# Four weight halves converted beside the attention and kept in memory, an integer mantissa, and a third bank for the first layer

## The chip, the core and the metric

The kernel runs on one core of one Trainium2 chip. Its engines work side by side, each on its own instructions in a fixed order: PE (TensorE) multiplies, PEld loads its weights, DVE (VectorE), ACT (ScalarE) and POOL (GpSimd) do element work, SP (SyncE) starts transfers. PE writes into eight PSUM banks of 128x512 floats, which DVE and ACT read and POOL does not use here. The metric is device time in microseconds; lower is better.

## The reference, cut to what matters

```python
B, H, S, D = 8, 8, 576, 64             # q, k, v; block-causal mask, blocks of 64
scores = q @ k.T / sqrt(D);  attn = softmax(mask(scores));  x = attn @ v
x = x.transpose(0, 2, 1, 3).reshape(4608, 512)
h = x @ w_in                            # w_in 512 x 2048
g = max(h, 0) + alpha * min(h, 0)       # alpha: one number for each of 2048 units
out = g @ w_out                         # w_out 2048 x 512
```

w_in and w_out come to the kernel as doubles. It has to make floats of them itself, with integer operations on the two 32-bit words of each double.

## The kernel before

**Stages.** The 32 pairs of heads (four to a batch of 576 tokens) run one after the other; the scores, softmax, transposes and values of each are `query_tile` and `values`. The 2048 hidden units are 16 blocks of 128, numbered f. For f = 0 to 5 both layers run in chunks of 256 tokens (`chunk_a`: `ffn1` at L518 for the first layer, `ffn2` at L555 for the second) beside the attention, and three of these chunks are left when it ends, near 598 us. Here they are called A chunks. Blocks 6 to 15 follow in nine chunks of 512 tokens (C chunks), two blocks at a time: `pair1` makes seven products of 128x256 (L596) and joins them on DVE (L605, L609); `activate` applies alpha (ACT L529, DVE L531, ACT L535, POOL L538); `ffn2` multiplies by w_out.

**Conversion.** `to_f32` turns one half (w_in or w_out of one f, 128x512) into floats. SP loads the doubles into `raw` (L414). DVE masks the exponent (L416), ACT scales it into a bank (L419), DVE adds the sign (L421) and masks the mantissa into a second bank (L425), ACT makes a float of that (L428), DVE adds the low word (L430) and multiplies by the exponent (L433) into `m`. So a half costs five DVE and two ACT instructions. Then `split` makes a high part on ACT (L438) and a low part on POOL (L439). There are two `raw` tiles, and two `m` tiles until the attention is over, then four.

**When.** The 12 halves of f = 0 to 5 are converted in the first 100 us (`first_weights`). Of the 20 later halves, w_in of f = 6 and 7 are converted early too (priority `SOON`, in the trace from 105.65 us on) and stay in the two `m` tiles. The other 18 are converted from 605 us to 707 us, beside the last three A chunks and the first C chunk (`later_weights`), together with w_in's sums on POOL (L455).

**Order.** All instructions are recorded with engine, cost and priority (`Plan.op`), and `Plan.schedule` lists them by a model of the costs: on each engine the ready instruction of lowest priority number goes first. The chip then runs each engine's list as it stands. Tiles and banks are claimed in this plan. Banks have quotas: 6 for attention (`att`), 1 for hidden values (`hp`), 1 for sums (`acc`) during the attention; after it `hp` is HT, `acc` is AM, and the conversions get WB = 4 (`words`).

```python
BANKS, HB, AB, HT, AM, AT, WB = 6, 1, 1, 2, 2, 4, 4
plan.quota["hp"] += HT - HB
```

Of the kernel before, what the change touches and what calls it, by code (L numbers as in the profile page):

```python
# [9 lines left out]
F32 = mybir.dt.float32  # L10
F32R = mybir.dt.float32r
BF16 = mybir.dt.bfloat16
I32 = mybir.dt.int32
U32 = mybir.dt.uint32
AF = mybir.ActivationFunctionType
ALU = mybir.AluOpType
# [4 lines left out]
NP = H // 2  # L21
NPAIR = B * NP
DM, DF, DO = H * D, 2048, 512
P = 128
NCC = DM // P
NF = DF // P
TOK = B * S
FA = 6
# [6 lines left out]
RING = 2 * S  # L35

HALVES = (((4, 3, 2), (2 * P, S, 1)), ((1, 0), (0, 2 * P, 0)))
BANKS, HB, AB, HT, AM, AT, WB = 6, 1, 1, 2, 2, 4, 4
C0, C1 = 3.0, 4.0
WARM, WARM_END = 10, 3400  # L40
TICK, FULL_COLUMNS, SP0 = 3413.33, 3060, 700
# [3 lines left out]
E0, E1 = -4.0, 1.0  # L45
FP = -1
XP = 2.0
SOON, XB = 150, 1006.7
FEW = 12
BEGIN = {"SP": SP0, "ACTQ": SP0, "POOLQ": SP0, "PE": WARM_END, "ACT": 2000, "DVE": 1500, "POOL": 1700}  # L50
# [177 lines left out]
def c_dve(n):  # L228
    return 65 + n / 0.96


def c_dve2(n):
    return 150 + n / 1.92


def c_act(n, sbuf=False):
    return (93 if sbuf else 51) + n / 1.2
# [35 lines left out]
def attn_ffn(ctx, tc, qT, kT, vT, w_in, w_out, alpha, out):  # L273
    nc = tc.nc

    const = ctx.enter_context(tc.tile_pool(name="const", bufs=1))
    dram = ctx.enter_context(tc.tile_pool(name="dram", bufs=1, space=bass.MemoryType.DRAM))
# [20 lines left out]

    xd = dram.tile([P, NCC, TOK], F32, name="xd")
    part = dram.tile([TOK, DO], F32, name="part")  # L300

    wraw = ctx.enter_context(tc.tile_pool(name="wraw", bufs=1))

# [8 lines left out]
    att = ExitStack()  # L312
# [36 lines left out]
    op = plan.op  # L349
# [52 lines left out]
    def to_f32(src, prio, after=(), use="att", early=None):  # L402

        raw, eb, fb, mb = Buf("raw"), Buf("bank", use), Buf("bank", use), Buf("m")

        def low():
            return raw().rearrange("p (n t) -> p n t", t=2)[:, :, 0].bitcast(U32)

        def high():
            return raw().rearrange("p (n t) -> p n t", t=2)[:, :, 1]  # L410

        def e():
            return eb().bitcast(I32)
        op("SP", 512, lambda: nc.sync.dma_start(out=raw(), in_=src), r=after, w=[raw], prio=prio if early is None else early)  # L414

        op("DVE", c_dve2(512), lambda: nc.vector.tensor_scalar(  # L416
            out=mb().bitcast(I32), in0=high(), scalar1=0x7FF00000, scalar2=None, op0=ALU.bitwise_and),
            r=[raw], w=[mb], claim=[fb, eb], prio=prio)
        op("ACT", c_act(512, True), lambda: nc.scalar.activation(  # L419
            out=e(), in_=mb().bitcast(I32), func=AF.Relu, bias=ebias, scale=8.0), r=[mb], w=[eb], prio=prio)  # L420
        op("DVE", c_dve(512), lambda: nc.vector.scalar_tensor_tensor(  # L421
            out=e(), in0=high(), scalar=-2 ** 31, in1=e(), op0=ALU.bitwise_and, op1=ALU.bitwise_or),
            r=[raw], w=[eb], prio=prio)

        op("DVE", c_dve(512), lambda: nc.vector.tensor_scalar(  # L425
            out=fb().bitcast(I32), in0=high(), scalar1=0xFFFFF, scalar2=0x100000, op0=ALU.bitwise_and, op1=ALU.bitwise_or),
            r=[raw], w=[fb], prio=prio)
        op("ACT", c_act(512), lambda: nc.scalar.activation(out=fb(), in_=fb().bitcast(I32), func=AF.Copy, scale=2.0 ** -20),  # L428
           w=[fb], prio=prio)
        op("DVE", c_dve(512), lambda: nc.vector.scalar_tensor_tensor(  # L430
            out=mb(), in0=low(), scalar=2.0 ** -52, in1=fb(), op0=ALU.mult, op1=ALU.add),
            r=[raw, fb], w=[mb], prio=prio)
        op("DVE", c_dve(512), lambda: nc.vector.tensor_tensor(out=mb(), in0=mb(), in1=eb(), op=ALU.mult), r=[eb], w=[mb], prio=prio)  # L433
        return mb, mb

    def split(src, hi, lo, n, r, hk, lk, claim, on, prio):
# [20 lines left out]

    w1s, w2s = {}, {}

    def later_weights(prio):  # L460


        for f in range(FA, NF, 2):
            W = w1s[f] = Buf("w1")

            ms = [to_f32(w_in[f + i].bitcast(I32), *((prio(f), ["att"], "words") if f > FA else (SOON, [], "att"))) for i in range(2)]
            (m0, w0), (m1, w1) = ms
            sb = Buf("ws")
            q11, q12 = ((m0, lambda j=j, w0=w0: w0()[:, 256 * j:256 * j + 256]) for j in range(2))
            q21, q22 = (((m1, j), lambda j=j, w1=w1: w1()[:, 256 * j:256 * j + 256]) for j in range(2))  # L470
            s1, s2 = (((sb, j), lambda j=j, sb=sb: sb()[:, 256 * j:256 * j + 256]) for j in range(2))
            pr = prio(f)
            add("POOL", 256, s1, q21, q22, ALU.add, pr, [m1, "att"])
            add("POOL", 256, s2, s1, q11, ALU.subtract, pr)
            add("POOL", 256, q21, q11, q21, ALU.subtract, pr)
            for src, r, at, n, on in ((w0, [m0, "att"], 0, 512, "POOL"), (w1, [m1, q21[0]], 2, 512, "POOL"),
                                      (lambda sb=sb: sb(), [s1[0], s2[0]], 4, 512, "POOL")):
                hi, lo = ((lambda x=x, at=at, n=n, W=W: W()[:, x, 256 * at:256 * at + n]) for x in range(2))
                split(src, hi, lo, n, r, (("w1", f, at), "h"), (("w1", f, at), "l"), [W], on, pr)
            add("POOL", 256, s2, q12, s2, ALU.subtract, pr)  # L480
            hi, lo = ((lambda x=x, W=W: W()[:, x, 6 * 256:]) for x in range(2))
            split(s2[1], hi, lo, 256, [s2[0]], (("w1", f, 6), "h"), (("w1", f, 6), "l"), [W], "POOL", pr)
            for i in range(2):
                W = w2s[f + i] = Buf("w2")
                mb, w = to_f32(w_out[f + i].bitcast(I32), prio(f) + .5, ["att"], "words")
                hi, lo = ((lambda x=x, W=W: W()[:, x, :]) for x in range(2))
                split(w, hi, lo, 512, [mb], (("w", f + i, 1), "h"), (("w", f + i, 1), "l"), [W], "POOL", prio(f) + .5)

# [496 lines left out]
    for p in range(NP):  # L985
        pr = E1 * (p - NP) + E0
# [6 lines left out]
    for p in range(NPAIR):  # L993
        if p == NV:
            op("NONE", 0, end_plain, ends=("vraw0",), prio=-100, then=lambda: rooms("pt", ("V", 1, [5, 4, D], F32R)),
               w=[("PT", i, h, j, x) for i in range(3) for h in range(2) for j in range(6) for x in range(2)])
        pr = p * 5
        qk_parts, v_parts = prep(p, pr - 4.5) if p else rest(pr - 4.5)
        k = 0
        for js, span in HALVES[:1] if p < NP else HALVES:  # L1000
            for j in js:
                query_tile(p, qk_parts, j, pr + k)
                k += 1
            values(p, v_parts, [span], pr + k + .5)
        if p % NP == NP - 1:
            b = p // NP
            spill(b, p * 5 + 20)
            if p == NPAIR - 1:
                break
            while done + CHA <= (b + 1) * S:  # L1010
                chunk_a(done)
                done += CHA
# [92 lines left out]
```

## Time and profile before

| | |
|---|---|
| median of 3 runs | 1147.3 us (1147.26 to 1149.0) |
| the profiled execution | 1147.15 us, of which its span is 1145.4 us |
| PE, PEld busy | 1119.7 us (98%), 999.0 us (87%) |
| DVE, ACT, POOL busy | 844.1 us (74%), 730.1 us (64%), 612.1 us (53%) |
| transfers | 145.86 MB, nearly all from SP's queue |

Read it by stretches: the start to about 110 us, the attention to 598 us, a passage from there to about 690 us in which the later weights are converted, and the C chunks to the end. The span is what the profile covers; the profiled execution's own time is 1.75 us longer. Matmuls overlap, so that a busy PE can be slower than PE at its best; the number of matmuls in a stretch tells more.

### The profile page before, as it was taken

To read this page: it belongs to the slowest core of one execution; us is meant where nothing else is said; L and a number is where in the kernel's file an instruction comes from. 1 tells how busy PE (TensorE), PEld (TensorE's weight loads), DVE (VectorE), ACT (ScalarE), POOL (GpSimd) and SP (SyncE) were. 2 spreads that over 40 slices of the span, in tenths; PEclk is the share of its full clock that TensorE was granted. 3 is DMA by queue.
4 is the path that set the end of the run, shared out by engine and by line. 5 is a ranking of instruction groups with operands and counts; after the bars stand their busy time and mean duration, and the time that the engine had idled before them with its cause. 6 is when DMAs were issued, how large, how long until landed. Compare 5 with 4: busy or idle time off the path is not lost. (4 is left out here: it accounts for less than half of the span.)

```text
span 1145.4 us, 22040 instructions
## 1 busy us (share of the span) xinstructions
PE 1119.7 (98%) x7288; PEld 999.0 (87%) x7288; DVE 844.1 (74%) x1968; ACT 730.1 (64%) x1950; POOL 612.1 (53%) x769
## 2 busy tenths in 40 slices
PE   7998999999999999999999989999999999999998
PEld 5666999999989999999998878988898889989887
DVE  8888899887887777778868999655657474656554
ACT  6887898987777887788865766443434343343432
POOL 5756556555565455556448987342425343342522
PEclk9999999999999999999999999999999999999999
DMA  8797676764745566557314442312122030302020
GB/s 229 218 258 234 172 215 175 205 176 113 228 133 151 163 180 183 132 142 226 88 48 165 144 143 74 116 37 74 41 71 78 34 111 1 111 16 95 2 74 37
DMA packets 74018, 145.86 MB, mean 127 GB/s; under 512 B 9648, under 2 KB 11440, under 8 KB 73904
## 3 DMA queue, kind: packets, MB, share of 16 engines
q1 hardware_dynamic: 73616, 144.31, 43.0%
q8 instruction: 58, 0.95, 0.4%
q14 instruction: 56, 0.46, 0.1%
q10 hardware_dynamic: 288, 0.14, 0.0%
HBM read 67.35 MB, written 28.31 MB: 84 GB/s over the span
## 5 line engine op out<-in xcount | busy, mean ns | idle before, releaser
L538 POOL TENSOR_TENSOR gl<-g,gh 128x256 fp32r<-128x256 f32 x288 | 223.2, 783 | 336.3 <-PE bank L596 159.6
L596 PEld LDWEIGHTS bank<-X,w 128*128 128x128 f32 x1890 | 253.6, 189 | 21.7 <-POOL X L439 1.1
L596 PE MATMUL bank<-X,w 128*128 128x256 f32 x1890 | 259.5, 281 | 1.3 <-POOL X L439 0.6
L555 PE MATMUL bank<-w,gh 128*128 128x512 f32 x720 | 225.8, 395 | 2.3 <-DVE g L531 1.3
L529 ACT ACTIVATE g<-bank 128x256 f32<-128x256 f32 x288 | 110.6, 385 | 158.2 <-DVE bank L609 142.0
L819 POOL TENSOR_SCALAR p<-p,ri 128x256 f32<-128x256 f32 (+3 forms) x256 | 146.0, 584 | 98.7 <-DVE ri L817 48.8
L535 ACT CAST gh<-g 128x256 fp32r<-128x256 f32 x288 | 116.9, 407 | 82.8 <-DVE g L531 81.6
L531 DVE SCALAR_TENSOR_TENSOR g<-g,oal,bank 128x256 f32<-128x256 f32 x288 | 136.0, 476 | 35.3 <-ACT g L529 29.4
L609 DVE TENSOR_TENSOR bank<-bank,g 128x256 f32<-128x256 f32 x180 | 76.0, 428 | 103.4 <-PE bank L596 102.4
L811 ACT ACTIVATE p<-bank,nm 128x256 f32<-128x256 f32 (+3 forms) x256 | 134.7, 531 | 27.0 <-DVE nm L808 11.8
L555 PE MATMUL bank<-w,gl 128*128 128x512 f32 x360 | 141.8, 394 | 1.4 <-POOL gl L538 1.4
L555 PE MATMUL bank<-wa,gh 128*128 128x512 f32 x432 | 140.9, 407 | 1.0 <-POOL wa L439 1.0
L555 PEld LDWEIGHTS bank<-w,gh 128*128 128x128 f32 x720 | 120.4, 188 | 15.4 <-DVE g L531 1.5
L518 PE MATMUL bank<-xh,wa 128*128 128x256 f32 x864 | 130.3, 288 | 0.0
L908 DVE TENSOR_TENSOR PL<-bank,PH 128x512 fp32r<-128x512 f32 (+2 forms) x189 | 111.1, 608 | 20.9 <-ACT PH L907 18.2
L518 PEld LDWEIGHTS bank<-xh,wa 128*128 128x128 f32 x864 | 114.1, 190 | 3.2 <-issue 0.4
L828 PE MATMUL bank<-ident,p 128*128 128x128 f32 x640 | 103.9, 280 | 6.6 <-POOL p L819 5.7
L795 PE MATMUL bank<-K,Q 128*128 128x512 f32 (+1 forms) x472 | 103.9, 335 | 0.0
L907 ACT CAST PH<-bank 128x512 fp32r<-128x512 f32 (+2 forms) x189 | 95.9, 529 | 11.8 <-PE bank L828 6.9
L828 PEld LDWEIGHTS bank<-ident,p 128*128 128x128 f32 x640 | 74.4, 142 | 19.7 <-POOL p L819 10.8
L605 DVE TENSOR_TENSOR g<-bank,g 128x256 f32<-128x256 f32 x135 | 56.6, 422 | 47.4 <-PE bank L596 46.5
L941 PE MATMUL bank<-PH,V 128*128 128x320 f32 x324 | 88.4, 288 | 0.0
(126 smaller groups left out, 2094.1 us busy)
## 6 DMA issues: line engine op xcount, KB each, us to landing
Q<-QH SPq DMA_DIRECT2D x62, 256.0 KB, 3.8
K<-KH SPq DMA_DIRECT2D x124, 128.0 KB, 3.6
vraw<-in_v SPq DMA_DIRECT2D x32, 320.0 KB, 3.1
qraw<-in_q SPq DMA_DIRECT2D x31, 320.0 KB, 3.6
xd<-xT SPq DMA_DIRECT2D x8, 1152.0 KB, 5.9
part<-o SPq DMA_DIRECT2D x36, 256.0 KB, 2.3
xb<-xd SPq DMA_DIRECT2D x9, 1024.0 KB, 5.3
m<-part SPq DMA_DIRECT2D x36, 256.0 KB, 3.3
```

What stands on the lines that cost most here:

```text
L518: nc.tensor.matmul(hp()[:, :n], ww()[:, 0, cc * P:(cc + 1) * P], x()[:, cc, :n], start=(i == 0 and cc == 0), stop=(i == 2 and cc == NCC - 1))
L529: op("ACT", c_act(CHA), lambda: nc.scalar.activation(out=g(), in_=hp()[:, ts], func=AF.Relu, scale=-1.0), r=[hp], w=[g], prio=FP)
L531: op("DVE", c_dve(CHA) + 60, lambda: nc.vector.scalar_tensor_tensor(out=g(), in0=g(), scalar=oal[:, f:f + 1], in1=hp()[:, ts], op0=ALU.mul ...
L535: op("ACT", c_act(CHA, True), lambda: nc.scalar.copy(out=gh(), in_=g()), r=[g], w=[gh], prio=FP)
L538: op("POOL", c_pool(CHA), lambda: nc.gpsimd.tensor_tensor(out=gl(), in0=g(), in1=gh().bitcast(F32), op=ALU.subtract), r=[g, gh], w=[gl], p ...
L555: nc.tensor.matmul(acc(), a()[:, ts], ww(), start=(first and i == 0), stop=(last and i == 2))
L596: nc.tensor.matmul(bank()[:, :CHA], W()[:, i, 256 * at + P * c:256 * at + P * c + P], B()[:, j, CHA * c:CHA * c + CHA], start=(n == 0), st ...
L795: nc.tensor.matmul(o, Q()[:, i, qs], K()[:, 2 * h + i, :w], start=(i == 0), stop=(i == 1))
L811: op("ACT", 238 + w / 1.2, lambda h=h, t=t: nc.scalar.activation(out=t()[:, :w], in_=sb[h]()[:, off[h]:off[h] + w], func=AF.Exp, bias=nm() ...
L819: op("POOL", 244 + w / 1.2, lambda h=h: nc.gpsimd.tensor_scalar(out=pts[h]()[:, :w], in0=pts[h]()[:, :w], scalar1=ri()[:, h:h + 1], scalar ...
L828: nc.tensor.transpose(out=tp()[:, base + c * P:base + (c + 1) * P], in_=pts[h]()[:, c * P:(c + 1) * P], identity=ident)
L908: op("DVE", c_dve(n) + (HALF if n == P else 0), lambda: nc.vector.tensor_tensor(out=lo(), in0=src(), in1=hi().bitcast(F32), op=ALU.subtrac ...
```

## The change

Four halves, w_in and w_out of f = 8 and f = 9, are no longer converted in the passage. `weights_ahead(p)` converts one after each of the pairs 12, 16, 20 and 24 and stores it to a DRAM tensor `wd`; `later` loads it from there into `m`. They still go through `split` and the sums on POOL. The ACT instruction that made a float of the mantissa is gone from all 32 conversions: DVE reads the integer in the bank directly, and the factors move into the two DVE instructions behind it. HT is 3.

```diff
-BANKS, HB, AB, HT, AM, AT, WB = 6, 1, 1, 2, 2, 4, 4
+BANKS, HB, AB, HT, AM, AT, WB = 6, 1, 1, 3, 2, 4, 4
+AHEAD = {(8 + k // 2, k % 2): 12 + 4 * k for k in range(4)}
...
+    wd = dram.tile([2 * (NF - FA), P, 512], F32, name="wd")
...
-        op("ACT", c_act(512), lambda: nc.scalar.activation(out=fb(), in_=fb().bitcast(I32), func=AF.Copy, scale=2.0 ** -20),
-           w=[fb], prio=prio)
         op("DVE", c_dve(512), lambda: nc.vector.scalar_tensor_tensor(
-            out=mb(), in0=low(), scalar=2.0 ** -52, in1=fb(), op0=ALU.mult, op1=ALU.add),
+            out=mb(), in0=low(), scalar=2.0 ** -32, in1=fb().bitcast(I32), op0=ALU.mult, op1=ALU.add),
             r=[raw, fb], w=[mb], prio=prio)
-        op("DVE", c_dve(512), lambda: nc.vector.tensor_tensor(out=mb(), in0=mb(), in1=eb(), op=ALU.mult), r=[eb], w=[mb], prio=prio)
+        op("DVE", c_dve(512), lambda: nc.vector.scalar_tensor_tensor(
+            out=mb(), in0=mb(), scalar=2.0 ** -20, in1=eb(), op0=ALU.mult, op1=ALU.mult), r=[eb], w=[mb], prio=prio)
...
+    def weights_ahead(p):
+
+        for f, i in (k for k in AHEAD if AHEAD[k] == p):
+            pr = 5 * p + 100
+            mb, _ = to_f32((w_in, w_out)[i][f].bitcast(I32), pr, [("x", p // NP % 2, p % NP, 0, 1)])
+            at = 2 * (f - FA) + i
+            op("SP", 256, lambda mb=mb, at=at: nc.sync.dma_start(out=wd[at], in_=mb()), r=[mb], w=[("wd", f, i)], prio=pr)
+
+    def later(f, i, prio, after=(), use="att"):
+        if (f, i) not in AHEAD:
+            return to_f32((w_in, w_out)[i][f].bitcast(I32), prio, after, use)
+        mb, at = Buf("m"), 2 * (f - FA) + i
+        op("SP", 256, lambda: nc.sync.dma_start(out=mb(), in_=wd[at]), r=[("wd", f, i), *after], w=[mb], prio=prio)
+        return mb, mb
...
-            ms = [to_f32(w_in[f + i].bitcast(I32), *((prio(f), ["att"], "words") if f > FA else (SOON, [], "att"))) for i in range(2)]
+            ms = [later(f + i, 0, *((prio(f), ["att"], "words") if f > FA else (SOON, [], "att"))) for i in range(2)]
...
-                mb, w = to_f32(w_out[f + i].bitcast(I32), prio(f) + .5, ["att"], "words")
+                mb, w = later(f + i, 1, prio(f) + .5, ["att"], "words")
...
             values(p, v_parts, [span], pr + k + .5)
+        weights_ahead(p)
```

`raw` and `m` tiles are given out in the order in which the program asks for them, so the `SOON` conversions of f = 6 and 7 now stand behind the four.

On SP, in the attention, the first of the four loads and its store stand among the loads and copies of the pairs' queries and keys (`raw` is the doubles, `wd` the new tensor, QH and KH are copied to Q and K). Now:

```order
L689 DMA kraw_246<-in_k 128x576
L416 DMA raw_167<-in_w_in 128x1024
L690 DMA vraw_171<-in_v 128x640
L675 DMA part<-o_154 128x512
L703 DMA Q_126<-QH_293 64x2x512 x2
L703 DMA Q_126<-QL_320 64x512 x2
L688 DMA qraw_235<-in_q 128x640
L703 DMA K_128<-KH_315 64x512 x4
L703 DMA K_128<-KL_326 64x512 x2
L689 DMA kraw_246<-in_k 128x576
L467 DMA wd<-m_228 128x512
L690 DMA vraw_171<-in_v 128x640
```

The load and the store are new; before, that place has only the other rows' kinds. Behind the store stand the next pair's values and then its copies.

On DVE, in the passage, behind the second conversion after the attention (w_out of f = 7 into `m_7465`) before the change:

```order
L430 SCALAR_TENSOR_TENSOR m_7465<-raw_256,bank_202 128x512
L416 TENSOR_SCALAR m_327<-raw_166 128x512
L433 TENSOR_TENSOR m_7465<-m_7465,bank_180 128x512
L425 TENSOR_SCALAR bank_221<-raw_166 128x512
L421 SCALAR_TENSOR_TENSOR bank_240<-raw_166,bank_240 128x512
L430 SCALAR_TENSOR_TENSOR m_327<-raw_166,bank_221 128x512
L433 TENSOR_TENSOR m_327<-m_327,bank_240 128x512
L416 TENSOR_SCALAR m_227<-raw_256 128x512
```

and now (the same half is `m_7471`; L547 is `activate` on DVE, which was L531; L440 and L456 make the C chunk's factors):

```order
L433 SCALAR_TENSOR_TENSOR m_7471<-m_7471,bank_188 128x512
L440 TENSOR_TENSOR X_7570<-xt_7562,X_7570 128x512
L427 TENSOR_SCALAR bank_241<-raw_167 128x512
L456 TENSOR_TENSOR xt_7562<-xb_7356,xt_7562 128x512
L427 TENSOR_SCALAR bank_222<-raw_257 128x512
L547 SCALAR_TENSOR_TENSOR g_724<-g_724,oal,bank_248 128x256
L547 SCALAR_TENSOR_TENSOR g_7426<-g_7426,oal,bank_203 128x256
L547 SCALAR_TENSOR_TENSOR g_7445<-g_7445,oal,bank_181 128x256
L547 SCALAR_TENSOR_TENSOR g_7465<-g_7465,oal,bank_188 128x256
```

Where the conversions of f = 8 and 9 followed at once, the layers' own instructions stand now, and the next conversion is that of f = 10.

On PE the A chunks of the passage stood interleaved before (here the last block of a chunk's first layer behind second-layer products):

```order
L518 MATMUL bank_187<-xl_448,wa_924 128x256 x4
L555 MATMUL bank_141<-wa_332,gh_504 128x512
L555 MATMUL bank_141<-wa_363,gh_504 128x512
L555 MATMUL bank_141<-wa_332,gl_516 128x512
L555 MATMUL bank_141<-wa_445,gh_634 128x512
L555 MATMUL bank_141<-wa_528,gh_634 128x512
L555 MATMUL bank_141<-wa_445,gl_641 128x512
L518 MATMUL bank_231<-xh_441,wa_1068 128x256 x4
```

and now (L534 and L571 are the old L518 and L555):

```order
L534 MATMUL bank_222<-xl_456,wa_862 128x256 x4
L534 MATMUL bank_203<-xh_443,wa_1022 128x256 x4
L534 MATMUL bank_203<-xh_443,wa_1037 128x256 x4
L534 MATMUL bank_203<-xl_456,wa_1022 128x256 x4
L571 MATMUL bank_142<-wa_337,gh_530 128x512
L571 MATMUL bank_142<-wa_361,gh_530 128x512
L571 MATMUL bank_142<-wa_337,gl_551 128x512
```

The six blocks of a chunk's first layer now stand in one piece, and its second layer behind them.

## Rows read from the trace of the kernel before

**Rows 1.** The page: busy time of the engines, then of PE and DVE by slices
```profile
PE 1119.7 (98%) x7288; PEld 999.0 (87%) x7288; DVE 844.1 (74%) x1968; ACT 730.1 (64%) x1950; POOL 612.1 (53%) x769
...
PE   7998999999999999999999989999999999999998
...
DVE  8888899887887777778868999655657474656554
```

**Rows 2.** Windows: each stretch, its length, busy time of each engine (instructions)
```profile
core 0: us, PE busy (x) PEld busy (x) DVE busy (x) ACT busy (x) POOL busy (x), PEclk, DMA share, GB/s
20.00:110.00 90.00, 82.25 (x457) 58.50 (x458) 77.81 (x188) 74.30 (x192) 59.19 (x67) 0.98 0.86 243
125.00:225.00 100.00, 99.25 (x717) 93.09 (x716) 90.06 (x243) 91.70 (x266) 59.41 (x85) 1.00 0.70 192
225.00:575.00 350.00, 347.48 (x2442) 322.81 (x2441) 281.76 (x715) 281.23 (x803) 202.06 (x276) 1.00 0.58 161
600.00:610.00 10.00, 10.00 (x62) 8.81 (x61) 5.12 (x10) 4.83 (x12) 8.97 (x12) 1.00 0.97 352
610.00:660.00 50.00, 48.29 (x292) 41.49 (x291) 47.51 (x75) 33.20 (x74) 44.23 (x45) 1.00 0.41 125
660.00:690.00 30.00, 24.95 (x156) 21.06 (x156) 29.10 (x56) 19.32 (x44) 25.38 (x25) 1.00 0.38 127
...
750.00:1100.00 350.00, 350.00 (x2196) 314.96 (x2195) 205.82 (x439) 139.84 (x346) 141.69 (x161) 1.00 0.18 61
```

**Rows 3.** Windows of PE's instructions alone: first L518, then L555, then L596
```profile
600.00:690.00 90.00, 26.69 (x216) 1.00 0.46 151
...
600.00:690.00 90.00, 44.36 (x174) 1.00 0.46 151
750.00:840.00 90.00, 55.16 (x209) 1.00 0.21 71
...
600.00:690.00 90.00, 15.92 (x116) 1.00 0.46 151
750.00:840.00 90.00, 48.79 (x354) 1.00 0.21 71
```

**Rows 4.** Groups on DVE, 600 to 720 us: first and last of five conversion lines
```profile
L416 DVE TENSOR_SCALAR m<-raw 128x512 int32<-128x512 int32 x18 | 12.6, 698 | 2.4 <-issue 2.4
...
L430 DVE SCALAR_TENSOR_TENSOR m<-raw,bank 128x512 f32<-128x512 uint32 x18 | 12.2, 679 | 0.5 <-ACT bank L428 0.5
```

**Rows 5.** Groups on ACT, 600 to 720 us: the conversion's two lines
```profile
L419 ACT ACTIVATE bank<-m,ebias 128x512 int32<-128x512 int32 x18 | 12.5, 692 | 9.4 <-DVE m L416 9.2
...
L428 ACT ACTIVATE bank<-bank 128x512 f32<-128x512 int32 x18 | 10.2, 568 | 0.0
```

**Rows 6.** Groups on POOL: 600 to 720 us, then one of 750 to 1100 us
```profile
L538 POOL TENSOR_TENSOR gl<-g,gh 128x256 fp32r<-128x256 f32 x41 | 34.5, 847 | 5.4 <-ACT gh L535 5.0 <-PE bank L518 0.3
L439 POOL TENSOR_TENSOR w<-m,w 128x512 fp32r<-128x512 f32 x20 | 26.8, 1341 | 8.6 <-ACT w L438 8.6
...
L538 POOL TENSOR_TENSOR gl<-g,gh 128x256 fp32r<-128x256 f32 x133 | 100.3, 767 | 193.7 <-PE bank L596 128.6 <-ACT gh L535 50.9 <-PE bank L555 10.3
```

**Rows 7.** The chain of waits in order of time, around 687 us: start, us, what
```profile
686.85 1.05 DVE m L416
688.34 0.97 PE bank L596 x6
690.71 2.76 PE bank L555 x12
```

**Rows 8.** Windows of 5 us in the start, columns as in Rows 2
```profile
85.00:90.00 5.00, 2.78 (x13) 1.89 (x12) 4.96 (x12) 4.18 (x11) 4.28 (x6) 0.86 0.95 269
90.00:95.00 5.00, 5.00 (x26) 3.49 (x24) 2.88 (x8) 4.17 (x11) 3.34 (x6) 0.80 0.97 383
...
105.00:110.00 5.00, 3.62 (x22) 2.67 (x22) 5.00 (x14) 4.42 (x13) 5.00 (x6) 1.00 1.00 282
```

**Rows 9.** Tile raw: DVE's first line, ns min/median/max, first and last start
```profile
L416 DVE TENSOR_SCALAR m<-raw x32: 410/502/1561, 11.2 to 703.3; 128x512 int32<-128x512 int32 x32
```

**Rows 10.** SP's own waits: total us, times, longest us
```profile
SPq L687 <- ACT KH L682: 44.5, 13, 8.6
```

**Rows 11.** The page, transfers: KB each, median us to landing
```profile
raw<-in_w_in SPq DMA_DIRECT2D x16, 512.0 KB, 4.0
```

## The prediction

> **What bounds the kernel now.** I read the page first: PE is busy 98% of the span and every slice but the first and a few later ones is full [rows 1], so the time is PE's work plus what PE loses. Next come the windows, to find where it loses. In the C chunks (750 to 1100 us) PE is never idle and DVE has two fifths of the time free; in the attention (125 to 225 and 225 to 575 us) PE is idle 0.75 of 100 us and 2.5 of 350 us [rows 2]. Two stretches remain: the passage from 600 to 690 us and the start, where PE is idle 7.75 us between 20 and 110 us [rows 2].
>
> For the passage I count matmuls. In a steady stretch of 90 us stand 354 of L596 (256 columns) and 209 of L555 (512 columns, twice the work): 354 + 418 = 772 units, 0.1166 us each. Between 600 and 690 us stand 216 + 116 of 256 columns and 174 of L555: 680 units, or 79.3 us of work in 90 us [rows 3]. **So PE loses 10.7 us there.** That is all that easing the passage can give. The Trainium skill says under "Identifying the Most-Contended Engine" (Perfetto Trace Analysis) that matmul busy time tells badly how close PE is to its limit and that LDWEIGHTS busy time tells it better; by busy PE the loss would be 6.8 us, by the skill's measure, 71.4 of 90 us against 315.0 of 350 us when steady, it is again 10.7 us [rows 2].
>
> What holds PE there: DVE is busy 76.6 of the 80 us from 610 to 690 us, POOL 69.6 [rows 2], and the chain of waits runs over DVE, at last over a conversion's L416 at 686.85 us, and from 688 us on over PE alone [rows 7]. So DVE is the bound until 688 us, and POOL is close behind it.
>
> **The change part by part.**
>
> *Four conversions leave the passage.* A half costs DVE five instructions of 0.679 to 0.698 us [rows 4], 3.43 us in all; four take 13.7 us. DVE was busy 5.1 + 76.6 us from 600 to 690 us and would be busy 68.0 us there, 86% of the 79.3 us that PE needs. In the attention DVE is busy 80% and 90% of the time while PE loses under 1% [rows 2]. By this count DVE stops being the bound.
>
> *POOL is late next.* The change takes nothing from POOL: split and sums of f = 8 and 9 stay. POOL was busy 9.0 + 44.2 + 25.4 = 78.6 of these 90 us [rows 2], so the stretch can't go under 78.6 us plus POOL's idle time, of which there were 11.4 us. A part of that ended on ACT, which waits for DVE's conversions (from 600 to 720 us 8.6 us before L439 and 5.0 us before L538) [rows 6], and gets shorter. I let half of it stay, 5.7 us: 84.3 us, a gain of 5.7 us. L538 takes 847 ns here and 767 ns in the C chunks [rows 6], 3.3 us over 41 of them; a quarter of that may go with the DVE work beside it, 0.8 us. **Passage: -6.5 us**, with 0 and -10.7 us as the ends.
>
> *One ACT instruction less in each conversion.* L428 takes 0.568 us [rows 5] and is removed 32 times: 14 of the removals stand in the conversions that remain in the passage, 8.0 us of ACT, and 12 in the start. With the L419 and L428 of the four moved halves (4 x 1.26 = 5.0 us) ACT gets 13.0 us lighter in a passage where it was not the bound; this is in the term above. The two DVE instructions that take over the factors keep shape and number. No row shows an integer in a bank read by this very form; L421 reads an integer bank in 0.69 us and L430 a float bank in 0.68 us, so I take 0, with 0.02 us as the other end.
>
> *The start.* Two conversions (f = 6 and 7) leave it: they begin at 105.65 us, where PE was idle 1.4 of 5 us with DVE and POOL full, and 12 x 0.57 = 6.8 us of ACT go. Before, PE was also idle 2.2 us from 85 to 90 us, and the granted clock fell to 0.86 and 0.80 of full in these two windows, which means that part of them ran at 1.2 instead of 2.4 GHz [rows 8], worth 5 x 0.14 + 5 x 0.20 = 1.7 us more. The ends are 0 and 7.75 + 1.7 = 9.4 us. The list of every engine is new there, so the losses will move as well as shrink. **I take -2.0 us**, near the row that the two conversions stand in.
>
> *Six conversions enter the attention.* The four and the two displaced ones add 6 x 3.4 = 21 us to DVE and 6 x 0.69 to ACT over 350 us: DVE goes from 80% to 86%, under the 90% at which PE lost 0.75 us in 100 [rows 2]. Each holds two of the six attention banks while it lasts. For that the nearest row is the start: 12 conversions beside 7.75 us of PE idleness, at most 0.65 us each, 3.9 us for six. The cover is that DVE is free for a fifth of the time and that the new work has the worst priority. **I take +0.7 us** (the idle rate of 125 to 225 us instead of that of 225 to 575 us, for a part of it), ends 0 and 3.9. The Trainium skill says in "SBUF — State Buffer", "Who interferes with whom", that POOL and DVE share a pair of ports and the second to issue is fully blocked; L416's 410 ns at best and 1561 ns at worst [rows 9] agree, and by that rule the moved L416s could meet POOL, busy 202 of 350 us there, and cost DVE up to 6 x 1.15 = 6.9 us more, which would leave it at 88% and the sum as it is.
>
> *Transfers.* Four stores and four loads of 256 KB are added, and four loads of 512 KB (about 4.0 us to landing [rows 11]) move into the attention, where the transfer engines are busy 58% of the time [rows 2]. In the passage a ready half of 256 KB replaces doubles of 512 KB. No instruction of SP's list is on the chain; 0 us, unless the stores hold the queue (last rival).
>
> *The third bank* lets PE do a chunk's first layer in one piece. It adds and removes no work; what it can save is stalls of the A chunks, and these are within the 10.7 us already. 0 us of its own.
>
> Sum against the profiled execution: 1147.15 - 6.5 - 2.0 + 0.7 = 1139.35 us. This execution lies 0.15 us under the median, 1147.3 us, so **1139.4 us** for the median.
>
> **The rivals.**
>
> *All of it.* DVE and ACT lighter, POOL's waits for them vanish, and PE runs the passage without a gap: -10.7 - 3 + 0.7, that is 1134 us. For it: DVE would be at 86%; against it: POOL at 78.6 of 79.3 us would have to be without a pause.
>
> *POOL takes DVE's place.* Of its idle 11.4 us 9 stay, since it waits for PE's products in turn. The passage gives 2.4 us, the start 1.5, the attention takes 0.7: 1144 us. For it: POOL's 87% there; against it: a third of its idle time ended on the conversions.
>
> *It doesn't do what it says.* If the passage is held by latencies of the first C chunk (product, join, activation) and not by DVE's load, the four halves bring nothing and the start's shuffle decides: 1147 us. Against it: DVE's 96% and the chain.
>
> *Slower: the stores hold SP's queue.* SP is one list; the store of a half waits for the conversion's last DVE instruction, which has the worst priority of all, and behind it stand the next pair's values and its copies of queries and keys, without which PE has no scores. SP already waits up to 8.6 us before such copies [rows 10]. It decides from the point where a conversion ends later than the copies' lead over PE. At 4 us of PE for each of four stores it costs 16 us, and with the gain of 7.8 us the time is 1155 us. Against it: the plan puts the store where it expects the conversion done, and in DVE's list the five instructions have other work between them to absorb a delay.
>
> **How the numbers follow.** Forecast 1139.4 us: 0.50. All of it, 1134 us: 0.17. POOL, 1144 us: 0.15. Nothing, 1147 us: 0.10. Slower, 1155 us: 0.08. A measurement of this kernel tells about 0.2%, 2.3 us, from no change, so faster means under 1145.0 us. Faster: 0.50 + 0.17 + 0.12 of POOL's 0.15 = 0.79. Same: the rest of POOL's and most of "nothing", 0.11. Slower: 0.08 and a little of "nothing", 0.10. The range, 1131.5 to 1147.5 us, takes in the first four, with the start's and the passage's gains some microseconds to either side; left out are the slower case and a larger gain in the start.
>
> **What would show it.** Right: between about 600 and 690 us PE's units rise from 680 to near 730, DVE's share falls under 90%, POOL's rises over 90%, and the chain leaves DVE earlier; fourteen conversions in the passage, six between 225 and 575 us with PE idle no more than 3 to 4 us there; in the start less idle PE around 85 to 110 us. Wrong: POOL's share unchanged with PE still waiting (POOL or latencies), scores that wait for copies after the pairs 12, 16, 20 and 24 (the stores), or a second fall of the granted clock.

## The result

The changed kernel takes 1135.4 us (median of 4 runs, 1134.2 to 1137.1); the kernel before took 1147.4 us in the same comparison (1147.3 to 1149.0). The ratio is 0.989, with a 95% interval of 0.988 to 0.991: 12.0 us faster, where 7.9 us were forecast and the range ended at 1131.5 us. The profiled execution took 1135.16 us with a span of 1133.4 us.

In the changed program L414 has become L416, L416 L418, L439 L440, L518 L534, L538 L554, L555 L571, L596 L612 and L687 L703. The page first, which answers to [rows 1]:

```profile
PE 1116.3 (98%) x7288; PEld 998.2 (88%) x7288; DVE 838.9 (74%) x1968; ACT 713.3 (63%) x1918; POOL 611.3 (54%) x769
```

The shares say almost nothing: they moved by a point at most. Next the windows, as in [rows 2] (length of the stretch, busy time and instructions of each engine, granted clock, transfer share):

```profile
core 0: us, PE busy (x) PEld busy (x) DVE busy (x) ACT busy (x) POOL busy (x), PEclk, DMA share, GB/s
20.00:110.00 90.00, 83.46 (x477) 59.12 (x477) 78.72 (x194) 70.33 (x189) 60.65 (x72) 1.00 0.87 237
125.00:225.00 100.00, 100.00 (x726) 94.39 (x725) 88.28 (x232) 89.49 (x257) 61.09 (x83) 1.00 0.69 191
225.00:575.00 350.00, 349.57 (x2449) 324.62 (x2448) 294.55 (x749) 286.43 (x811) 200.66 (x276) 1.00 0.61 170
600.00:610.00 10.00, 10.00 (x80) 9.73 (x79) 7.92 (x15) 8.14 (x20) 9.97 (x12) 1.00 0.77 250
610.00:660.00 50.00, 48.01 (x293) 41.60 (x291) 42.24 (x67) 28.94 (x63) 46.67 (x46) 1.00 0.41 119
660.00:690.00 30.00, 29.53 (x188) 26.32 (x188) 29.42 (x60) 17.12 (x42) 26.07 (x29) 1.00 0.29 100
```

Two things stand here. In the attention PE's idle time went from 2.5 to 0.4 us in 350, although six conversions came into it and DVE's busy time rose by 12.8 us (281.8 to 294.6 us). In the passage DVE fell to 79.6 of 90 us (88%) and POOL rose to 82.7 (92%): these are the two shares that the prediction named. Then PE's products from 600 to 690 us, first L534, then L571, then L612, as in [rows 3]:

```profile
600.00:690.00 90.00, 26.23 (x216) 1.00 0.41 127
...
600.00:690.00 90.00, 42.68 (x173) 1.00 0.41 127
...
600.00:690.00 90.00, 22.70 (x168) 1.00 0.41 127
```

In units of 256 columns that is 216 + 2 x 173 + 168 = 730 where it was 680, the number that the prediction gave. The chain of waits has left DVE for POOL in the middle of the passage, where [rows 7] had conversions on it until 686.85 us (start, us, what):

```profile
646.24 1.62 POOL gl L554 x2
647.86 0.70 POOL ws L456
648.56 3.40 POOL w L440 x3
...
654.53 4.35 POOL X L440 x3
...
663.63 1.25 POOL w L440
664.89 1.40 POOL gl L554 x2
666.29 2.95 POOL w L440 x2
669.24 1.16 POOL ws L456
670.40 1.85 POOL gl L554 x2
...
682.73 0.98 PE bank L612 x6
```

**A ledger for all kernels.** The products in all are the same in every kernel here, so two numbers of a trace say where its time went: the work still left at 600 us (units after 600 us, at the prediction's 0.1166 us) and the loss after 600 us (span minus 600 minus that work). Before, 4536 units or 528.9 us were left and 16.5 us were lost, of which 5.3 us lie behind 690 us (5.1 to 5.9 us in most of the kernels below, more where a stall falls behind 690 us). After, 4484 units or 522.8 us were left and 10.6 us were lost. **So the 12.0 us are 6.1 us won before 600 us and 5.9 us won behind it, in the passage.** The prediction had -1.3 and -6.5 us.

### The profile page after: what moved, and what is told of

Same layout as the page of the kernel before. It is cut to its first block, busy times and chain, and to the rows that moved or that the text cites. A ratio compares the mean times of both kernels' runs of the same rounds, so it can differ in the third digit from the quotient of the medians.

```text
span 1133.4 us, 22046 instructions
## 1 busy us (share of the span) xinstructions
PE 1116.3 (98%) x7288; PEld 998.2 (88%) x7288; DVE 838.9 (74%) x1968; ACT 713.3 (63%) x1918; POOL 611.3 (54%) x769
## 4 chain that ended last, share of the span: by engine, by line
PE 87%; POOL 4%; DVE 4%; DMA 2%; ACT 1%; issue 1%; SPq 0%; POOLq 0%; DVEq 0%; ACTq 0%
PE bank L571 32%; PE bank L612 18%; PE bank L534 11%; PE bank L957 7%; PE bank L811 6%; PE bank L844 6%; PE bank L947 2%; PE bank L874 2%; PE bank L901 1%; POOL w L440 1%; POOL gl L554 1%; POOL p L835 1%; DMA raw<-in_w_in 1%; POOL ws L456 1%; ACT p L827 0%
## 5 line engine op out<-in xcount | busy, mean ns | idle before, releaser
L554 POOL TENSOR_TENSOR gl<-g,gh 128x256 fp32r<-128x256 f32 x288 | 220.1, 773 | 337.0 <-PE bank L612 169.8
L612 PEld LDWEIGHTS bank<-X,w 128*128 128x128 f32 x1890 | 253.7, 189 | 22.2 <-POOL X L440 2.4
L612 PE MATMUL bank<-X,w 128*128 128x256 f32 x1890 | 259.4, 281 | 2.2 <-POOL X L440 1.7
L571 PE MATMUL bank<-w,gh 128*128 128x512 f32 x720 | 225.6, 394 | 0.0
L547 DVE SCALAR_TENSOR_TENSOR g<-g,oal,bank 128x256 f32<-128x256 f32 x288 | 136.0, 476 | 41.2 <-ACT g L545 35.0
L571 PE MATMUL bank<-w,gl 128*128 128x512 f32 x360 | 141.7, 394 | 0.0
L571 PE MATMUL bank<-wa,gh 128*128 128x512 f32 x432 | 141.2, 408 | 0.0
L571 PEld LDWEIGHTS bank<-w,gh 128*128 128x128 f32 x720 | 120.4, 188 | 12.8 <-DVE m L430 0.2
L534 PE MATMUL bank<-xh,wa 128*128 128x256 f32 x864 | 130.0, 288 | 0.8 <-ACT wa L439 0.4
L534 PEld LDWEIGHTS bank<-xh,wa 128*128 128x128 f32 x864 | 114.2, 190 | 4.6 <-DVE g L547 1.1
```

The source lines that it names most:

```text
L534: nc.tensor.matmul(hp()[:, :n], ww()[:, 0, cc * P:(cc + 1) * P], x()[:, cc, :n], start=(i == 0 and cc == 0), stop=(i == 2 and cc == NCC - 1))
L547: op("DVE", c_dve(CHA) + 60, lambda: nc.vector.scalar_tensor_tensor(out=g(), in0=g(), scalar=oal[:, f:f + 1], in1=hp()[:, ts], op0=ALU.mul ...
L554: op("POOL", c_pool(CHA), lambda: nc.gpsimd.tensor_tensor(out=gl(), in0=g(), in1=gh().bitcast(F32), op=ALU.subtract), r=[g, gh], w=[gl], p ...
L571: nc.tensor.matmul(acc(), a()[:, ts], ww(), start=(first and i == 0), stop=(last and i == 2))
L612: nc.tensor.matmul(bank()[:, :CHA], W()[:, i, 256 * at + P * c:256 * at + P * c + P], B()[:, j, CHA * c:CHA * c + CHA], start=(n == 0), st ...
```

## The experiments

The first theory, A: the four halves carry the passage, start and attention gain through lighter lists, the third bank does nothing. Against it stood that the mantissa or the third bank carry a part, and that the new order of the lists makes the difference rather than any work. One profile, and one order of the lists, stands behind each ledger row; a kernel's executions lie mostly within 2 us of their median (a few up to 5 us away), so differences of a microsecond say nothing.

| kernel | time, us (before beside it) | ratio, 95% interval | work left at 600 us | loss after 600 us |
|---|---|---|---|---|
| before | 1147.4 | | 528.9 | 16.5 |
| mantissa alone | 1149.0 (1147.6) | 0.999 to 1.002 | 527.7 | 18.1 |
| third bank alone | 1150.5 (1147.6) | 1.001 to 1.003 | 528.2 | 20.2 |
| mantissa and bank | 1147.4 (1147.5) | 0.999 to 1.001 | 528.0 | 17.8 |
| halves alone | 1143.9 (1147.6) | 0.995 to 0.997 | 524.7 | 16.7 |
| halves and mantissa | 1138.8 (1147.6) | 0.989 to 0.993 | 522.6 | 14.9 |
| halves and bank | 1141.4 (1147.5) | 0.993 to 0.997 | 526.8 | 12.9 |
| all three (the change) | 1135.4 (1147.4) | 0.988 to 0.991 | 522.8 | 10.6 |
| before, LONGER 1.13 | 1148.5 (1147.5) | 1.000 to 1.002 | 527.7 | 16.8 |
| before, LONGER 1.11 | 1146.5 (1147.5) | 0.998 to 1.000 | 527.3 | 18.2 |
| changed, LONGER 1.13 | 1142.7 (1147.5) | 0.993 to 0.997 | 528.0 | 12.9 |
| changed, LONGER 1.11 | 1143.1 (1147.5) | 0.994 to 0.997 | 530.2 | 11.2 |
| before, f = 6 and 7 late | 1146.8 (1147.5) | 0.999 to 1.001 | 526.8 | 17.9 |
| changed, eight halves | 1136.6 (1147.5) | 0.989 to 0.993 | 524.5 | 10.7 |

### The three parts, one at a time and in pairs

*Mantissa alone.* From the kernel before:

```diff
-        op("ACT", c_act(512), lambda: nc.scalar.activation(out=fb(), in_=fb().bitcast(I32), func=AF.Copy, scale=2.0 ** -20),
-           w=[fb], prio=prio)
```

with the factors in the two DVE instructions as in the change.

> The kernel before, with the integer mantissa alone: the ACT instruction is gone from all 32 conversions, no half goes ahead, the bank quota stays 2. Theory A (the four halves ahead carry the passage, the start gains from both the lighter ACT and the displaced conversions of f = 6 and 7): start -2 to -3 us, passage 0 to -2 us, 1143 to 1145 us. Theory B (the mantissa carries the start's whole gain of about 6 us): 1141 us, with the last values product of the attention at 585 to 586 us instead of 591.0. Theory C (the order of the new plan, not any part, makes the difference): anything between 1142 and 1149 us, without a stretch that explains it.

Measured: no change. At 600 us 1.2 us less work was left, where B expected a gain of about 6 us, and what PE loses in the passage is no smaller. Theory B falls, A's 1143 to 1145 us are missed too, and the time lies in C's range alone.

*Halves alone.* `AHEAD`, `weights_ahead` and `later` as in the change; the ACT instruction and the quota of 2 stay.

> The kernel before, with the four halves converted ahead and kept in memory alone: the ACT instruction on the mantissa stays, the bank quota stays 2. Theory A: passage -5 to -6 us with its units from 600 to 690 us near 720 (680 before, 730 with the whole change), start -3 us because f = 6 and 7 are displaced: 1138 to 1140 us. Theory B (the mantissa carries the start): passage -6 us alone, 1141 us, with the last values product still near 591 us. Theory C: 1142 us or more.

Measured: 3.7 us faster, all of it before 600 us. **In the passage nothing was won (16.7 us lost, 16.5 before), although DVE was relieved as planned:**

```profile
600.00:690.00 90.00, 84.25 (x510) 72.81 (x509) 77.45 (x130) 57.09 (x130) 80.22 (x83) 0.98 0.43 139
```

DVE is busy 77.5 of 90 us (81.7 before), POOL 80.2 (78.6 before). Theory A's central step fails here, and B's with it, since both gave the passage 5 to 6 us; the time is that of C (1142 us or more). The passage did not open when DVE alone got lighter. This is one order of the lists; other orders of one kernel moved the loss after 600 us by 2 us (below).

*Third bank alone.*

```diff
-BANKS, HB, AB, HT, AM, AT, WB = 6, 1, 1, 2, 2, 4, 4
+BANKS, HB, AB, HT, AM, AT, WB = 6, 1, 1, 3, 2, 4, 4
```

> The kernel before, with the third bank for the first layer alone. Theory A: no work goes, DVE stays the bound of the passage, 1146 to 1148 us. Rival (the third bank lets the A chunks run without stalls and carries the passage): 1141 to 1143 us, units from 600 to 690 us over 710.

Measured: 2.9 us slower, 0.2%. The rival's sign came (720 units, over 710), but not its time, and A's 1146 to 1148 us are missed on the other side. Until 690 us PE ran ahead, and then it stood: from 690 to 750 us it was idle for 5.6 us and ran partly at the lower clock level (0.94 of full granted on average). The windows:

```profile
600.00:690.00 90.00, 87.02 (x546) 76.16 (x545) 81.06 (x146) 59.81 (x135) 77.79 (x82) 1.00 0.43 142
690.00:750.00 60.00, 54.41 (x315) 48.16 (x314) 41.19 (x82) 27.04 (x63) 32.20 (x34) 0.94 0.30 97
```

And the wait of PE from 600 to 740 us that belongs to it (us in total, times, longest us):

```profile
PE bank L596 <- POOL w L439: 5.6, 2, 3.4
```

The bank let PE use up its A chunks sooner, and then the C chunk's weights were not there. The stall was put off, not removed.

*The change without the third bank:* HT back to 2.

> The changed kernel with the quota of the first layer back at 2. Theory A: the start stays as it is with the whole change and the passage too, 1135 to 1137 us. Rival (the third bank carries a part of the passage that opens only once DVE is lighter): 1138 to 1141 us, with units from 600 to 690 us back under 715.

Measured: 1138.8 us, 3.5 us above the change. The work left at 600 us is the same (522.6 and 522.8 us), so the whole difference lies in the passage: a loss of 14.9 us instead of 10.6. The rival is right, and the prediction's "0 us of its own" is wrong. The two kernels side by side from 600 to 690 us, first without the bank, then with it: the windows, and then the waits of PE's weight loads for `gl`.

```profile
600.00:690.00 90.00, 85.55 (x526) 74.35 (x525) 79.00 (x135) 53.76 (x122) 83.37 (x85) 0.98 0.42 133
```

```profile
600.00:690.00 90.00, 87.54 (x557) 77.65 (x556) 79.59 (x140) 54.20 (x125) 82.71 (x85) 1.00 0.41 127
```

The waits, in the same order:

```profile
PEld bank L571 <- POOL gl L554: 5.1, 10, 1.0
```

```profile
PEld bank L571 <- POOL gl L554: 1.9, 5, 0.6
```

DVE and POOL are equally busy in both, within 0.7 us. What differs is how long the second layer's products wait for `gl`, which POOL makes: 5.1 us in ten waits, or 1.9 us in five. With three banks PE has more of a first layer to do while POOL works, and finds `gl` ready when it comes. That the waits fell is shown; that the number of free banks is what lets PE go on is read from the new order, and not measured by itself.

*Halves and bank, without the mantissa; mantissa and bank, without the halves.*

> The kernel before with the four halves ahead and the third bank, but with the ACT instruction on the mantissa left in. Each trace gives two numbers: the products still to be done at 600 us (528.9 us of work before, 522.8 with the whole change, 524.7 with the halves alone), and what PE loses after 600 us (16.5 before, 10.6 with the whole change, 16.7 with the halves alone, 14.9 without the third bank). Theory A (the third bank opens the passage once DVE is lighter): 524 to 525 us of work left, loss after 600 us 11 to 13 us, 1137 to 1139 us. Rival B (the passage needs ACT lighter as well): loss near 16 us, 1142 to 1144 us.

> The kernel before with the integer mantissa and the third bank, and no half ahead. Theory A (the third bank pays only once DVE has lost the four halves): loss after 600 us 17 to 21 us as with the bank alone (20.2) or the mantissa alone (18.1), 1148 to 1151 us. Rival B (any relief of the conversions lets the third bank pay): loss 12 to 14 us, 1142 to 1144 us.

Measured: 12.9 and 17.8 us lost after 600 us, which is what theory A gave for each; the times, 1141.4 and 1147.4 us, lie outside its ranges (1137 to 1139 and 1148 to 1151 us), the first because 526.8 us of work were left at 600 us instead of 524 to 525. Without the halves no combination goes under 16 us lost (16.5, 18.1, 20.2, 17.8). With them the bank takes off 3.8 us without the mantissa (16.7 to 12.9) and 4.3 us with it (14.9 to 10.6); the mantissa takes off 1.8 and 2.3 us.

Why the parts need each other shows when the loss is split at 690 us (products that straddle 690 us count on both sides, so the two parts can miss the sum by 0.5 us):

| loss, us: 600 to 690, behind 690 | with two banks | with three banks |
|---|---|---|
| neither halves nor mantissa | 10.7, 5.3 | 6.0, 13.7 |
| mantissa | 12.3, 5.3 | 7.3, 10.4 |
| halves | 10.9, 5.3 | 5.8, 6.9 |
| halves and mantissa | 9.3, 5.2 | 4.9, 5.2 |

The third bank takes 4.4 to 5.1 us off the stretch up to 690 us in every row, with the halves or without them. With the bank alone DVE was busy 81.1 of these 90 us, as before (81.7 us), and PE did 720 units in place of 680: so it was not DVE's load that held PE to 680 units there. The halves matter behind 690 us. Without them the bank's gain is lost again, because PE comes to the C chunk before its weights are there: it waited 5.6 us for POOL's `w` with the bank alone, and with the mantissa beside it

```profile
PE bank L595 <- POOL w L438: 2.6, 3, 2.0
```

from 690 to 750 us. In the four kernels of the table with the halves ahead no wait of PE for `w` is listed there (at LONGER 1.13, further below, there are 2.1 us of it). **The bank wins the time and the halves keep it; alone neither brings a gain in the passage.**

### How much is the order?

LONGER is a factor of the planner's cost model; no instruction of the program depends on it, only the order in which they are listed.

```diff
-LONGER = 1.12
+LONGER = 1.13
```

First the changed kernel with 1.13 (and, further below, 1.11):

> The changed kernel with one figure of the planner's model changed by 1% (LONGER, the factor on its costs, 1.12 to 1.13), which gives another order and the same work: how much the order alone is worth. If the gain comes from the work: 1135 us within 2 us, loss after 600 us 10 to 12 us. If much of it is a lucky order: 1139 us or more, with a loss of 14 us or more.

Measured: 1142.7 us, 7.3 us more than the change as it was given, with the same work. Of this, 5.2 us were lost before 600 us (528.0 instead of 522.8 us left) and 2.3 us behind. The time is that of a lucky order (1139 us or more); the loss of 12.9 us lies between the two forecasts (10 to 12, 14 or more). So I asked the same of both kernels.

> The kernel before with LONGER at 1.13 instead of 1.12: the same work in another order. After the changed kernel lost 7 us by the same step, theory A is that the order alone moves either kernel by some us and that the change is worth about 4 to 5 us in the passage whatever the order: then this gives 1144 to 1152 us, work left at 600 us 526 to 530 us, loss after 600 us 16 to 20 us. Rival B (the kernel before had an unlucky order and the change little worth): 1138 to 1143 us, loss after 600 us 11 to 14 us.

> The kernel before with LONGER at 1.11: a third order of the old work. Theory A: 1144 to 1152 us with a loss after 600 us of 16 to 20 us. Rival B: 1138 to 1143 us with 11 to 14 us.

> The changed kernel with LONGER at 1.11: a third order of the new work. Theory A (the passage's gain is the change's, the gain before 600 us is the order's): loss after 600 us 10 to 14 us, work left at 600 us anywhere from 522 to 529 us, 1135 to 1143 us. Rival C (both gains are the work's and the 1.13 was the unlucky one): work left near 523 us, loss near 11 us, 1134 to 1137 us.

Measured: the kernel before stays within 1146.5 to 1148.5 us in its three orders; the changed one takes 1135.4, 1142.7 and 1143.1 us. The order that was given is the best of its three by 7 us, and that is luck: nothing in the change chose it. Where the other two lose it shows in two windows, 20 to 60 us and 225 to 575 us, in the order given, then at 1.13, then at 1.11:

```profile
20.00:60.00 40.00, 37.90 (x214) 26.50 (x213) 36.09 (x92) 30.64 (x85) 25.56 (x32) 1.00 0.89 234
225.00:575.00 350.00, 349.57 (x2449) 324.62 (x2448) 294.55 (x749) 286.43 (x811) 200.66 (x276) 1.00 0.61 170
```

```profile
20.00:60.00 40.00, 35.85 (x201) 24.83 (x202) 33.85 (x86) 29.01 (x78) 27.66 (x34) 1.00 0.84 233
225.00:575.00 350.00, 347.07 (x2426) 321.45 (x2425) 294.59 (x741) 285.06 (x808) 205.42 (x274) 1.00 0.61 172
```

```profile
20.00:60.00 40.00, 33.17 (x179) 23.66 (x178) 35.77 (x89) 29.10 (x78) 27.43 (x33) 0.96 0.87 228
225.00:575.00 350.00, 347.52 (x2435) 322.08 (x2434) 293.61 (x743) 282.74 (x805) 201.23 (x274) 1.00 0.62 174
```

PE loses 2.1 and 4.7 us more in the start, and 2.5 and 2.1 us more in the attention. DVE's busy time in the attention is the same within 1 us in all three, so it is not the amount of work that the six conversions bring that differs there; where they stand in the lists may. By the means of three orders each:

- work left at 600 us: 528.0 us before, 527.0 us after, and the three orders of after lie 7.4 us apart. Nearly all of the 6.1 us won before 600 us came with this order. How much of it the change gives in general is open: the seven kernels without halves ahead left 526.8 to 528.9 us, the seven with them 522.6 to 530.2 us;
- loss after 600 us: 17.2 us before (16.5 to 18.2), 11.6 us after (10.6 to 12.9). **The gain of 5.6 us in the passage is the change's: no order of before loses less than 16.5 us, none of after more than 12.9 us.**

By the means of the three medians the change is worth 7.1 us (1147.5 to 1140.4 us). Theory A as it was put for these runs holds, but for the 530.2 us left at 1.11, which lie over its 522 to 529 us; its rivals (an unlucky order of before; 1.13 as the single unlucky one) fall. Three orders are few, and how far a fourth would lie stays open.

### Do the displaced conversions of f = 6 and 7 carry the start?

Only the argument that differs is shown:

```diff
-... (SOON, [], "att") ...
+... (SOON, [("x", 0, 1, 0, 1)], "att") ...
```

> The kernel before with one thing moved: the conversions of w_in of f = 6 and 7 don't begin at 105 us but late in the attention; all work stays. Theory A (what the halves ahead gained before 600 us, 4.2 us, came from these two leaving the start): work left at 600 us 525 us, loss after 600 us 16 to 17 us, 1143 us. Rival B (it came from the other order of the attention): work left 528 to 529 us, 1147 us.

Measured: they did move, from 105.65 and 107.27 us to 493.87 and 508.73 us (DVE's timeline, start and us):

```profile
493.87 0.42 DVE L416 TENSOR_SCALAR m<-raw 128x512 int32<-128x512 int32 x1
508.73 0.42 DVE L416 TENSOR_SCALAR m<-raw 128x512 int32<-128x512 int32 x1
```

The work left at 600 us is 2.1 us smaller (526.8 us, between the two forecasts), the loss after it 1.4 us larger (17.9 us, over both), and the time is B's, that of before. So these two leaving the start explain at most half of the 4.2 us that the halves alone gained before 600 us, and no gain in the time came with it. As three orders of the changed kernel lie 7.4 us apart there, no cause can be read from this single run.

### Is POOL the next bound?

```diff
-AHEAD = {(8 + k // 2, k % 2): 12 + 4 * k for k in range(4)}
+AHEAD = {(8 + k // 2, k % 2): 8 + 3 * k for k in range(8)}
```

> The changed kernel with eight halves ahead (f = 8 to 11) instead of four, after the pairs 8, 11 and so on to 29. DVE loses another 13.7 us in the passage, POOL nothing. Theory A (POOL is the passage's bound once four halves are gone): POOL over 90% from 600 to 690 us, loss after 600 us not under 10 us, 1134 to 1140 us. Rival B (DVE is still the bound): loss 6 to 8 us, and 1131 to 1133 us if the attention keeps its 523 us of work left at 600 us.

Measured: 1136.6 us and a loss of 10.7 us after 600 us, as with four. POOL is busy 80.7 of 90 us, 89.6%, just short of theory A's 90%; its time and its loss came. First the window from 600 to 690 us, then its chain of waits:

```profile
600.00:690.00 90.00, 88.38 (x556) 78.10 (x555) 63.44 (x116) 50.35 (x116) 80.65 (x83) 1.00 0.42 138
```

```profile
654.68 1.30 POOL X L440
656.68 1.69 POOL X L440
...
664.72 1.25 POOL w L440
665.97 1.45 POOL gl L554 x2
667.42 3.01 POOL w L440 x2
...
671.53 2.34 POOL gl L554 x2
```

DVE is down from 79.6 to 63.4 us and it buys nothing; the chain runs over POOL's `X`, `w` and `gl` from 654.7 up to 673.9 us. DVE is not the bound; that POOL is one is suggested by its share and by the chain, and not shown. A kernel that takes work from POOL in the passage was not tried. Eight halves do not beat four.

## Why the prediction was right, and where it was not

**The sum.** 12.0 us came where 7.9 us were forecast. By the ledger the passage is -5.9 us (forecast -6.5) and what lies before it -6.1 us (forecast -2.0 + 0.7).

**The bound, and four conversions leave the passage.** The count holds: of the 10.7 us lost from 600 to 690 us 5.8 us came back (4.9 us lost after: 90 minus 730 x 0.1166). The forecast's signs came: units of 730, DVE at 88%, POOL at 92%, fourteen conversions (the first begins at 599.19 us), the chain on POOL from 646 to 672 us, then ten microseconds nearly all on DVE, and from 682.7 us on over PE (688.34 us before). The mechanism was wrong in part. "So DVE is the bound until 688 us" fails on the bank alone, where DVE was as busy and PE did 720 units. And the step "By this count DVE stops being the bound" did not give the 5.7 us that were written beside it: with the halves alone DVE was 4.3 us lighter, and 10.9 us were still lost up to 690 us. The size (-6.5 us forecast, -5.9 us measured) was right for the three parts together and was put down to one of them; that it came so near is luck.

**POOL is late next.** Right in the main: POOL's idle time in the 90 us fell from 11.4 to 7.3 us, and its busy time rose from 78.6 to 82.7 us. Its waits for ACT's casts of the weights, in [rows 6] 8.6 us from 600 to 720 us, fell to 1.3 us. But the 5.0 us before L538, which the prediction also put down to the conversions, wait for `gh`, a cast of `activate` that depends on no conversion, and rose to 7.3 us. The prediction also let L538 get quicker beside a lighter DVE. It went from 847 to 814 ns:

```profile
L554 POOL TENSOR_TENSOR gl<-g,gh 128x256 fp32r<-128x256 f32 x43 | 34.4, 814 | 11.1 <-ACT gh L551 7.3 <-PE bank L612 3.8
L440 POOL TENSOR_TENSOR w<-m,w 128x512 fp32r<-128x512 f32 x19 | 25.2, 1327 | 1.3 <-ACT w L439 1.3
```

**The third bank, 0 us of its own.** Wrong. It is worth 3.8 and 4.3 us of the passage where the halves are ahead; without them it cost 3.7 us alone and brought 0.3 us beside the mantissa. The argument was that it removes no work; but the stalls it saves, 4.4 to 5.1 us up to 690 us, are most of what the passage's term consisted of.

**The mantissa.** No gain alone, neither in the passage, where the prediction had said that ACT was not the bound, nor in the start, where it had counted 6.8 us of ACT among its reasons. With the halves 1.8 and 2.3 us, which is as much as two orders of one kernel differ, so this part is not settled. The integer bank costs nothing: L430 takes 678 to 679 ns as in [rows 4].

**The start, -2.0 us.** This is the term that was mis-sized in the number, and the kind of term was wrong too. Start and attention together gave -6.1 us, against -1.3 in the sum. The signs named for it came; PE was idle 0.7 instead of 3.6 us from 85 to 110 us, without a fall of the clock, against [rows 8], though over the whole of 20 to 110 us only 6.5 instead of 7.75 us, since other losses came in:

```profile
85.00:90.00 5.00, 5.00 (x34) 3.59 (x33) 4.12 (x9) 2.88 (x8) 4.44 (x7) 1.00 0.93 304
...
105.00:110.00 5.00, 4.69 (x35) 4.17 (x34) 4.58 (x12) 4.10 (x12) 5.00 (x7) 1.00 0.20 43
```

But two other orders of the same work left 0.9 us less and 1.3 us more than before at 600 us. The sentence "the losses will move as well as shrink" was the right one; the ends of 0 and 9.4 us gained should have taken in a loss of a few microseconds.

**Six conversions enter the attention, +0.7 us.** They cost nothing that can be seen: with DVE at 84% PE is idle 0.4 us from 225 to 575 us, and 2.9 and 2.5 us in the other two orders, against 2.5 us before. The +0.7 us does not follow from the rows that it named: their idle rates, 0.75 us in 100 and 2.5 us in 350, differ by 0.1 us over 350 us. (And the sum's 1139.35 us plus 0.15 us is 1139.5 us, not 1139.4.)

The Trainium skill's rule in "SBUF — State Buffer", "Who interferes with whom", which was weighed for this step and which the page states for DVE's 2-port modes, found nothing to block there: all six L418 began while POOL ran no instruction, and took 414 ns on average. In the passage the traces agree with it, instruction by instruction (last section); the mean there is 959 ns, against 698 ns in [rows 4]. DVE's groups, first 225 to 575 us, then 600 to 720 us:

```profile
L418 DVE TENSOR_SCALAR m<-raw 128x512 int32<-128x512 int32 x6 | 2.5, 414 | 0.0
```

```profile
L418 DVE TENSOR_SCALAR m<-raw 128x512 int32<-128x512 int32 x13 | 12.5, 959 | 2.9 <-DMA raw<-in_w_out 2.2 <-POOL w L440 0.6
```

**The rivals.** *Slower: the stores hold SP's queue* fell. SP did wait before the stores, 11.6 us in three waits from 225 to 600 us, up to 7.5 us, and PE waited for no copy behind them; in the whole of 225 to 575 us its one listed wait is 0.2 us. SP's wait first, then PE's:

```profile
SPq L467 <- DVE m L433: 11.6, 3, 7.5
```

```profile
PE bank L811 <- ACT pl L887: 0.2, 1, 0.2
```

*It doesn't do what it says* is true of the four halves alone in the passage (16.7 us lost). *POOL takes DVE's place* is what the passage looks like, at a better price than the 2.4 us of that rival. *All of it* was near the time (1134 us), but not for its reason: 4.9 us are still lost from 600 to 690 us, and the rest of the gain came from before 600 us.

## What to carry to other kernels

Where a planner or a compiler sets the order, run both versions in a few other orders before you put a gain down to the edit: here some 7 of 12 us came with the order, and one constant of the cost model, changed by 1%, took them away. When two engines stand within a few per cent of each other in the stretch that loses time, relieving the busier one alone may bring nothing; count what the other one and the buffers between them allow, and cost the edits as a set. Split the loss before you name its cause: here the bank let PE run ahead, and the halves saw to it that the next stage's weights were there. Work left at a fixed time and loss behind it, both in units of the bounding engine's work, place a gain that shares of busy time don't show.

## What the runs showed of the hardware that was not expected

How long DVE's masking of doubles from `raw` into `m` (L418) takes depends on whether a POOL instruction is running when it begins. Of the 13 from 600 us on, the one that met an idle POOL took 0.43 us; each of the other twelve lasted until POOL's instruction was over, and 0.28 to 0.29 us more. Two of them, each behind the POOL instruction that it met (start, us, what):

```profile
632.69 1.29 POOL L440 TENSOR_TENSOR w<-m,w 128x512 fp32r<-128x512 f32 x1
632.76 1.50 DVE L418 TENSOR_SCALAR m<-raw 128x512 int32<-128x512 int32 x1 [2.22 <-DMA raw<-in_w_out]
```

```profile
679.05 1.29 POOL L440 TENSOR_TENSOR w<-m,w 128x512 fp32r<-128x512 f32 x1 [1.08 <-ACT w L439]
679.17 1.46 DVE L418 TENSOR_SCALAR m<-raw 128x512 int32<-128x512 int32 x1
```

In the traces of all fourteen kernels this instruction met a POOL instruction with more than 0.15 us to run 269 times, and 256 times it ended 0.28 to 0.29 us behind that one. The other 13 took 0.40 to 0.43 us, as beside an idle POOL; ten of them began within 0.05 us of POOL's start. So its mean does not follow POOL's share: it took 959 ns with POOL busy 92% of 600 to 690 us, but 823 ns with 93% in the change without the third bank, and with LONGER at 1.13 three of the six in the attention met POOL and took 494, 910 and 939 ns. The conversion's L423, L427 and L430, which read or write a bank, kept to 666 to 708 ns in the whole run.

So a part of DVE's busy time is waiting for POOL: at 0.42 us each the 13 would have taken 5.5 us, and 7.0 us of their 12.5 us went on it; in the kernel before it was 5.0 us of the 12.6 us of 18.
